# Output copies ahead of products at block seams, filter loads entered in another order, and a constant table in two parts

## The chip, the cores and the metric

One Trainium2 chip, one of its cores. The metric is the device time of one execution in microseconds (us), as the median of several; the lower the better. A profile of one execution of each kernel was taken as well.

## The reference

A frequency-domain mixing layer (a two-dimensional transform of `x`, an elementwise product with a learned complex filter, the transform back) is followed by RMS normalisation and a SwiGLU feed-forward without bias. Cut to what matters:

- `x` is 8 batches of 3008 rows (64 x 47) of 256 columns in single precision; the output has 24064 rows of 256.
- mix: transform, times `filt_r + i filt_i`, transform back, real part;
- norm: `y / sqrt(mean(y^2) + 1e-6) * moe_rms_g`;
- feed-forward: `(silu(y @ w_gate) * (y @ w_val)) @ w_out`.

## The kernel before

In the views PE is TensorE, PEld its weight load, DVE VectorE, ACT ScalarE, POOL GpSimd and SP SyncE; PSUM is the memory that matmuls write their sums to, here in banks.

The feed-forward fills TensorE: each block (batch `b`, `m`) is 12 "slots", one for each 128 columns of the hidden layer. The transforms of the *next* batch are cut into small units, which are put into the slots: stage A (`a_unit`), stage B with the filter products (`b_unit`, and for most units two half-swaps, `swap_unit`), the inverse (`bi_unit`), the normalisation (`n_unit`, `sq_unit`, `q_unit`). Where a unit stands in a slot decides its place in the order of each engine:

```python
def at(slot, fn, *a):
    todo = {q_unit: late, swap_unit: pre}.get(fn, plan).setdefault(slot, [])
    ...
for i in range(len(items) + 4):
    for fn, a in pre.get(i, ()):   fn(*a)       # half-swaps
    if i < len(items):             gv(*items[i])     # gate and value of slot i: 4 matmuls, silu, product hh
    for fn, a in plan.get(i, ()):  fn(*a)       # most units
    if 2 <= i < len(items) + 2:    down(*items[i - 2])   # output matmuls of slot i - 2
    for fn, a in late.get(i, ()):  fn(*a)
```

`down` of a block's last slot, which falls in a slot that is 1 modulo 12 (the "seam"), also copies the finished output out of PSUM: ScalarE one half, VectorE the other. The next block's matmuls into the same bank wait for these copies.

After batch 0, stage B has one PSUM bank. Its readers are, in this order, the product `s1` and the two half-swaps; the second half-swap frees the bank for the next unit:

```python
def b_unit(b, i, ps=None):
    if ps is None:
        ps = b_mm(b, i)                     # 2 matmuls into the single bank "mb"
    ...
    if summed(b, i):
        nc.vector.tensor_tensor(out=s1, in0=ps, in1=f1, op=ALU.mult)
        return
    eng.tensor_tensor(out=s1, in0=ps, in1=f1, op=ALU.mult)
    eng.tensor_tensor(out=s2, in0=ps, in1=f2, op=ALU.mult)

def swap_unit(b, i, h):                     # at slots s0 + 1 (h = 0) and s0 + 2 (h = 1)
    if h:
        nc.vector.tensor_tensor(out=s2[a], in0=ps[e], in1=f2[e], op=ALU.mult)
    else:
        nc.vector.scalar_tensor_tensor(out=s2[a], in0=ps[e], scalar=-1.0, in1=f2[e], ...)
    if h:
        nc.gpsimd.tensor_tensor(out=s, in0=s1, in1=s2, op=ALU.add)
```

Inverse units, stage A and most of the normalisation share another single bank, "mx". The kernel's eight banks are all in use (gate 2, value 2, output 2, "mx", "mb").

The start, where the loads are issued. `x` is cast on its way and is issued by GpSimd, in eight pieces; the real filters are issued by SP once GpSimd has zeroed the half of `fr` that lies under them:

```python
nc.sync.dma_start(tb, tab["tb"])            # constants, 224 KB
nc.sync.dma_start(wbp, tab["wbp"])
for c in range(NXC):
    x_load(0, c)                            # two loads each, by GpSimd
nc.gpsimd.memset(fi[0][HALF:P], 0.0)
nc.gpsimd.memset(fr[0][0:HALF], 0.0)
...
for c in range(4):
    f_load(c, 0, nc.sync)                   # real filters: 4 issues for c = 0
    f_load(c, 1, nc.gpsimd if c < 3 else nc.sync)   # imaginary filters
```

Of the kernel before, what the change touches and what calls it, by code (L numbers as in the profile page):

```python
# [11 lines left out]
FP16 = mybir.dt.float16  # L12
# [8 lines left out]
P = 128  # L21
# [3 lines left out]
JT = DFF // P  # L25
# [13 lines left out]
def _make_tables():  # L39
    n2 = np.arange(N2)  # L40
    wa = np.zeros((P, P))
    wai = np.zeros((P, P))
    for h in range(2):
        for k2 in range(K2):
            c = np.cos(2 * np.pi * ((n2 * k2) % N2) / N2)
            s = np.sin(2 * np.pi * ((n2 * k2) % N2) / N2)
            r = slice(h * 64, h * 64 + 64)
            wa[r, h * 64 + k2] = c
            wai[h * 64 + k2, r] = c * (1.0 if k2 == 0 else 2.0)
            if k2 == 0:  # L50
                alt = 1.0 - 2.0 * (n2 % 2)
                wa[r, h * 64 + 32] = alt
                wai[h * 64 + 32, r] = alt
            else:
                wa[r, h * 64 + 32 + k2] = -s
                wai[h * 64 + 32 + k2, r] = -2.0 * s
    n1 = np.arange(N1)
    wb = np.zeros((KR, K2, P))
    wi = np.zeros((P, 1, 2, P))
    re, im = slice(0, N1), slice(SL, SL + N1)  # L60
    for k2 in range(K2):
        for s in range(48):

            if s < 24:
                k = k2 + 64 * s
                sign, q = 1.0, 16 + 2 * s
            else:
                if k2 and s == 36:
                    continue
                j = s - 23 if (s < 36 or not k2) else s - 24  # L70
                k = 64 * j - (k2 if k2 else 32)
                sign, q = -1.0, 1 + 2 * (s - 24)
            th = 2 * np.pi * ((n1 * k) % N) / N
            c, sn = np.cos(th), np.sin(th)
            if k == 0 or k == NF - 1:
                sn = np.zeros(N1)
            if k2:
                wb[re, k2, q] = c
                wb[im, k2, q] = sign * sn
                wb[re, k2, HALF + q] = -sn  # L80
                wb[im, k2, HALF + q] = sign * c
            else:
                src = re if s < 24 else im
                wb[src, k2, q] = c
                wb[src, k2, HALF + q] = -sn
                m = 1.0 if k in (0, NF - 1) else 2.0
                z = np.zeros(N1)
                g = (m * c, -m * sn)
                gr, gi = (g, (z, z)) if s < 24 else ((z, z), g)


                for qq, cols in ((re, 0), (im, 1)):
                    wi[q, 0, 0, qq] = (gr, gi)[cols][0]
                    wi[HALF + q, 0, 0, qq] = (gr, gi)[cols][1]
                    wi[q, 0, 1, qq] = (gr, gi)[cols][1]
                    wi[HALF + q, 0, 1, qq] = (gr, gi)[cols][0]
    f = np.float16
    wf = np.zeros((P, K2, P))
    wf[:, 1:, 0:KR] = wb[:, 1:].transpose(2, 1, 0)
    wf[:, 0] = wi[:, 0, 0]  # L100
    wf = (wf * S_INV_B).astype(f)
    ws = np.concatenate([wf[HALF:P], -wf[0:HALF]], 0)
    wai = (wai * S_INV_A).astype(f)
    r = np.arange(KR)
    to_row = (r % 2) * SL + (r // 2 % 2) * H + r // 4
    pm = np.zeros((KR, P))
    pm[r, to_row] = 1.0
    k = np.arange(P)
    ph = (k % 2) * 64 + (k // 2 % 2) * 32 + k // 4
    tb = np.zeros((P, 7, P), f)  # L110
    tb[:, 0] = wa
    tb[:, 1] = np.eye(P)
    tb[0:KR, 2] = pm * S_INV_B
    tb[:, 3] = wf[:, 0]
    tb[:, 4] = ws[:, 0]
    tb[:, 5] = wai[ph]
    tb[:, 6] = wa[:, ph]
    return {"tb": tb, "wb": wb.astype(f), "wbp": wb[to_row].astype(f)}


@with_exitstack
def kernel(
# [11 lines left out]
    nc = tc.nc  # L134
# [9 lines left out]
    glob = ctx.enter_context(tc.tile_pool(name="glob", bufs=1))  # L144
# [12 lines left out]
    psM = ctx.enter_context(tc.tile_pool(name="psM", bufs=1, space=bass.MemoryType.PSUM))  # L157
    psB = ctx.enter_context(tc.tile_pool(name="psB", bufs=1, space=bass.MemoryType.PSUM))

    tb = glob.tile([P, 7, P], FP16)  # L160
    wa, ident, wai, wa2 = (tb[:, i, :] for i in (0, 1, 5, 6))
    pm = tb[0:KR, 2, :]
    sgn = glob.tile([P, 1], FP32)
    wi = glob.tile([P, 2, K2, P], FP16)
# [58 lines left out]
        return fr[c][:, r:r + n, :], fi[c][:, r:r + n, :]  # L223

    def wi_at(q, k):
        return wi[:, q, k, :] if k else tb[:, 3 + q, :]

    def b_mm(b, i):
        ps = bank(3 if b else (0, 3, 4, 5)[i % 4], "psb").rearrange("p (a d) -> p a d", a=2)
# [9 lines left out]
        return ps  # L239

    def summed(b, i):
        return b > 1 or b == 1 and i in (6, 7, 10, 11, 14, 15)

    def b_unit(b, i, ps=None):
        if ps is None:
            ps = b_mm(b, i)
        f1, f2 = filt(2 * i, 2)
        if b:
            s1 = late_p["sp"].tile([P, 2, D], FP16, tag="s1", name="s1")
            s2 = late_p["sp"].tile([P, 2, D], FP16, tag="s2", name="s2")  # L250
            if summed(b, i):
                nc.vector.tensor_tensor(out=s1, in0=ps, in1=f1, op=ALU.mult)  # L252
                st[b]["s"][i] = (s1, s2, ps, f2)
                return
        elif i % 2:
            s1 = hp.tile([P, 512], FP16, tag="sg", name="sg").rearrange("p (a d) -> p a d", a=2)
            s2 = hhs[(i // 2) % 4].rearrange("p (a d) -> p a d", a=2)
        else:
            ss = xnp.tile([P, 2, 512], FP16, tag="xn", name="ss")
            s1, s2 = (ss[:, e, :].rearrange("p (a d) -> p a d", a=2) for e in range(2))  # L260
        eng = nc.vector
        if (i in (3, 5, 8, 12)) if b else (i in (3, 7, 9, 12)):
            eng = nc.gpsimd
            v = yp.tile([P, 2, 512], FP32, tag="y", name="v")
            v = v[:, 0, :].rearrange("p (a d) -> p a d", a=2)
            nc.scalar.activation(out=v, in_=ps, func=AXT.Copy)
            ps = v
        eng.tensor_tensor(out=s1, in0=ps, in1=f1, op=ALU.mult)
        eng.tensor_tensor(out=s2, in0=ps, in1=f2, op=ALU.mult)  # L269
        st[b]["s"][i] = (s1, s2)  # L270
# [229 lines left out]
    def f_load(c, e, eng):  # L500
        lo = 1 if c == 0 else 0
        src, t, p0 = ((filt_r, fr[c], 0), (filt_i, fi[c], HALF))[e]
        eng.dma_start(t[p0 + 16:p0 + 63:2, :, :].rearrange("p a d -> p (a d)"),
                      raw(src, c * KC, [[64 * D, 24], [1, KC * D]]))
        for g in range(2):
            eng.dma_start(t[p0 + 1 + 24 * g:p0 + 24 + 24 * g:2, lo:KC, :],
                          raw(src, 64 * (1 + 11 * g) - c * KC - lo,
                              [[64 * D, 12], [-D, KC - lo], [1, D]]))
        if c == 0:
            eng.dma_start(t[p0 + 1:p0 + 48:2, 0, :], raw(src, 32, [[64 * D, 24], [1, D]]))  # L510
# [122 lines left out]
    with tc.manual_schedule():  # L633
# [18 lines left out]
        for c in range(NXC):  # L652
            x_load(0, c)
        nc.gpsimd.memset(fi[0][HALF:P], 0.0)
        nc.gpsimd.memset(fr[0][0:HALF], 0.0)
        nc.vector.memset(aT[:, 2 * H:, :], 0.0)
        nc.vector.memset(ones, 1.0)
# [6 lines left out]
            nc.sync.dma_start(gsb, moe_rms_g.rearrange("(a p) -> p a", p=P))  # L664
        for c in range(4):
            f_load(c, 0, nc.sync)
            f_load(c, 1, nc.gpsimd if c < 3 else nc.sync)

        warm_up(14, 1)
        for g in range(4):  # L670
# [130 lines left out]
        pre, plan, late = {}, {}, {}  # L801

        def at(slot, fn, *a):
            todo = {q_unit: late, swap_unit: pre}.get(fn, plan).setdefault(slot, [])
            if fn == sq_unit:
                todo.insert(0, (fn, a))
            else:
                todo.append((fn, a))

        def norm_plan(b, m, s0, s1, r):  # L810
            for dh in range(2):
                at((s0, s1)[dh], n_unit, b, m, dh)
                at((s0, s1)[dh] + 1, sq_unit, b, m, dh)
            steps = (q_unit, rho_load, xn_unit)
            if halved(b, m):
                at(s1 + 2, fold_unit, b, m)
                r = (4, 8, 12)
            if (b, m) in by_matmul:
                steps = (q_unit, scale_split, scale_apply)
            for d, fn in zip(r, steps):  # L820
                at(s1 + d, fn, b, m, *((3,) if fn == scale_apply else ()))
# [9 lines left out]
        for b in range(1, B):  # L831
# [6 lines left out]
            if b == 1:  # L838
                a_at = [8, 9, 9, 10, 10, 11, 11, 12, 12, 13, 13, 14]
                on_dve = (2, 4, 6, 8, 10)  # L840
                b_at = [22 + 7 * i // 4 for i in range(16)]
                lag, t4_at = 4, 55
                n_at, n_step = [58, 62, 66, 86, 95, 107], 3
            elif b == 2:
                a_at = [51, 52, 53, 53, 54, 54, 57, 57, 58, 59, 60, 61]
                on_dve = (0, 1, 3, 5, 7, 8, 9, 10, 11)
                b_at = [71 + 3 * i for i in range(16)]
                lag, t4_at = 5, 123
                n_at = [127 + 8 * m for m in range(6)]
            elif b == 3:  # L850
                b_at[0] += 1
                a_at = [77, 78, 80, 81, 83, 84, 92, 93, 101, 102, 104, 105]
# [72 lines left out]
```

## Time and profile before

| | |
|---|---|
| median of 4 runs | 893.5 us (892.68 to 894.44) |
| span of the profiled core | 890.6 us |
| TensorE waits for the VectorE output copy | 3.0 us, 6 times |
| ScalarE begins its first copy of the real filters | 20.99 us |
| TensorE's granted clock | full from 4 to 888 us |

From the page of the profiled execution, busy time and share of the span of each engine:

```profile
PE 873.5 (98%) x6258; PEld 559.4 (63%) x6258; DVE 681.5 (77%) x1091; ACT 625.1 (70%) x1068; POOL 435.6 (49%) x392
...
L276 DVE TENSOR_TENSOR s<-psb,fi 64x512 f16<-64x512 f32 x102 | 69.8, 684 | 3.1
```

TensorE (PE) is busy 98%: a change to VectorE's (DVE) order can only be worth the few TensorE gaps that it closes. The second line is the second half-swap: 102 times, 0.684 us each; VectorE hardly ever waits ahead of it (3.1 us in all).

### The profile page before, as it was taken

How to read it: one execution, taken by the hardware profiler on the slowest of the kernel's cores; microseconds unless marked ns; L12 is line 12 of the kernel's file. 1: busy time of each engine (PE TensorE's matmuls, PEld its weight loads, DVE VectorE, ACT ScalarE, POOL GpSimd, SP SyncE). 2: the span in 40 equal slices, each digit the busy share in tenths (PEclk: the TensorE clock that was granted, in tenths of full speed). 3: DMA queues.
4: the chain of work that ended last, by engine and by line, in shares of the span. 5: the costliest groups of instructions: out<-in, count | busy, mean ns of one | idle time of the engine just before them, and what ended most of it. 6: DMA issues, size and time to landing. Idle time of an engine off the chain costs nothing.

```text
span 890.6 us, 17468 instructions
## 1 busy us (share of the span) xinstructions
PE 873.5 (98%) x6258; PEld 559.4 (63%) x6258; DVE 681.5 (77%) x1091; ACT 625.1 (70%) x1068; POOL 435.6 (49%) x392
## 2 busy tenths in 40 slices
PE   8799999999999999999999999999999999999997
PEld 5666666666666666666666666666666666666556
DVE  7866787889987877888688787888878887555555
ACT  7877657677677766877677766787657765676444
POOL 7843830656427661677236662376515762155300
PEclk9999999999999999999999999999999999999999
DMA  8696726675663456335645247233352232222202
GB/s 196 122 196 156 157 67 207 143 158 110 162 159 89 101 111 185 107 90 113 159 119 132 86 81 199 80 94 90 88 163 72 67 90 61 85 66 49 72 24 48
DMA packets 80095, 101.44 MB, mean 114 GB/s; under 512 B 8108, under 2 KB 56684, under 8 KB 79560
## 3 DMA queue, kind: packets, MB, share of 16 engines
q1 hardware_dynamic: 69688, 84.23, 34.8%
q0 software_dynamic: 10240, 15.96, 11.4%
q8 instruction: 49, 0.80, 0.4%
q14 instruction: 38, 0.31, 0.1%
q10 hardware_dynamic: 80, 0.13, 0.1%
HBM read 67.67 MB, written 46.78 MB: 129 GB/s over the span
## 4 chain that ended last, share of the span: by engine, by line
PE 87%; issue 4%; DVE 2%; ACT 2%; DMA 2%; POOL 2%; SPq 0%; ACTq 0%; POOLq 0%; DVEq 0%
PE po L462 26%; PE pg L443 25%; PE pv L443 25%; PE psi L291 3%; PE psb L238 3%; PE psn L323 2%; PE psa L203 2%; DMA fr<-in_filt_r_dram 1%; DVE o L469 1%; ACT fr L516 1%; DVE hh L448 1%; DMA rb<-r_tmp 1%; ACT gT L578 1%; PE psq L352 0%; POOL xc L188 0%
## 5 line engine op out<-in xcount | busy, mean ns | idle before, releaser
L448 DVE TENSOR_TENSOR hh<-pv,sg 128x512 f16<-128x512 f32 (+2 forms) x588 | 392.9, 670 | 190.2 <-ACT sg L447 77.6
L447 ACT ACTIVATE sg<-pg 128x512 f16<-128x512 f32 (+2 forms) x588 | 340.9, 580 | 227.5 <-PE pg L443 217.8
L462 PE MATMUL po<-wo,hh 128*128 128x256 f16 x2244 | 343.2, 272 | 3.8 <-DVE o L469 3.0
L443 PE MATMUL pv<-xn,wv 128*128 128x512 f16 (+2 forms) x1176 | 339.6, 370 | 0.0
L443 PE MATMUL pg<-xn,wg 128*128 128x512 f16 (+2 forms) x1176 | 339.5, 370 | 0.0
L462 PEld LDWEIGHTS <-hh 128*128 128x128 f16 x2256 | 216.4, 98 | 99.0 <-issue 5.3
L282 POOL TENSOR_TENSOR s<-s,s 128x512 f16<-128x512 f16 x102 | 117.9, 1157 | 237.5 <-DVE s L276 165.6
L443 PEld LDWEIGHTS <-wv 128*128 128x128 f16 x1176 | 114.9, 98 | 128.8 <-issue 0.3
L419 POOL TENSOR_TENSOR xn<-y,rb 128x1024 f16<-128x1024 f32 (+1 forms) x45 | 126.0, 2801 | 44.9 <-DMA rb<-r_tmp 37.7
L443 PEld LDWEIGHTS <-wg 128*128 128x128 f16 x1176 | 111.4, 98 | 13.0 <-issue 0.3
L358 POOL TENSOR_TENSOR rho<-u,mhalf 128x4 f32<-128x4 f32 (+1 forms) x48 | 49.1, 1022 | 63.5 <-DVE u L356 63.1
L276 DVE TENSOR_TENSOR s<-psb,fi 64x512 f16<-64x512 f32 x102 | 69.8, 684 | 3.1
L296 ACT ACTIVATE t<-psi 96x512 f16<-96x512 f32 x112 | 66.4, 593 | 8.1 <-PE psi L291 2.7
L278 DVE SCALAR_TENSOR_TENSOR s<-psb,fi 64x512 f16<-64x512 f32 x102 | 70.7, 693 | 1.4
L252 DVE TENSOR_TENSOR s<-psb,fr 128x512 f16<-128x512 f32 x102 | 69.4, 681 | 0.0
L329 ACT ACTIVATE y<-psn,gsb 128x512 f32<-128x512 f32 (+1 forms) x94 | 63.8, 679 | 7.8 <-PE psn L323 0.5
L343 POOL TENSOR_TENSOR sq<-sq 128x512 f16<-128x512 f16 (+1 forms) x35 | 39.6, 1133 | 35.9 <-ACT sq L335 35.9
L335 ACT ACTIVATE sq<-psn 128x512 f16<-128x512 f32 (+1 forms) x94 | 54.8, 583 | 0.0
L208 ACT ACTIVATE t<-psa 128x512 f16<-128x512 f32 x70 | 41.8, 597 | 5.6 <-PE psa L203 2.4
L291 PE MATMUL psi<-s,wi 128*128 128x256 f16 x236 | 44.1, 273 | 0.0
L238 PE MATMUL psb<-t,wb 96*128 96x256 f16 x224 | 43.0, 272 | 0.5 <-DVE s L269 0.5
L323 PEld LDWEIGHTS <-t 128*128 128x128 f16 x368 | 28.4, 98 | 20.6 <-issue 0.4
(104 smaller groups left out, 523.1 us busy)
## 6 DMA issues: line engine op xcount, KB each, us to landing
out_dram<-o SPq DMA_DIRECT2D x83, 256.0 KB
xc<-in_x_dram POOLq DMA_DIRECT2D x56, 192.0 KB, 5.8
z_tmp<-t SPq DMA_DIRECT2D x28, 384.0 KB
t<-z_tmp SPq DMA_DIRECT2D x28, 384.0 KB
g_tmp<-t SPq DMA_DIRECT2D x56, 192.0 KB
rb<-r_tmp SPq DMA_DIRECT2D x41, 256.0 KB
t<-g_tmp SPq DMA_DIRECT2D x21, 384.0 KB
t<-g_tmp SPq DMA_DIRECT2D x7, 320.0 KB
```

The lines of the kernel that those rows point to most:

```text
L238: nc.tensor.matmul(ps[:, u, :], w[:, k, :], t, start=True, stop=True)
L252: nc.vector.tensor_tensor(out=s1, in0=ps, in1=f1, op=ALU.mult)
L276: nc.vector.tensor_tensor(out=s2[a], in0=ps[e], in1=f2[e], op=ALU.mult)
L278: nc.vector.scalar_tensor_tensor(out=s2[a], in0=ps[e], scalar=-1.0, in1=f2[e], op0=ALU.mult, op1=ALU.mult)
L282: nc.gpsimd.tensor_tensor(out=s, in0=s1, in1=s2, op=ALU.add)
L291: nc.tensor.matmul(ps[:, u, :], wi_at(q, 2 * i + u), ss[q][:, u, :], start=(q == 0), stop=(q == n - 1))
L296: nc.scalar.activation(out=st[b]["t3"][c][:, 2 * r:2 * r + 2, :], in_=ps[0:KR], func=AXT.Copy)
L419: nc.gpsimd.tensor_tensor(out=xv, in0=yv, in1=rv.unsqueeze(1).to_broadcast([P, 2, n, P]), op=ALU.mult)
L443: nc.tensor.matmul(ps[:, 0:w], wt[:, dt_, ts(jt, P)], xn[:, dt_, :], start=(dt_ == 0), stop=(dt_ == 1))
L447: nc.scalar.activation(out=sg[:, 0:w], in_=pg[:, 0:w], func=AXT.Silu)
L448: nc.vector.tensor_tensor(out=hh[:, 0:w], in0=pv[:, 0:w], in1=sg[:, 0:w], op=ALU.mult)
L462: nc.tensor.matmul(po[s4 // per][:, s4 % per, :], hh[:, ts(s4, P)], wo[:, jt, :], start=(jt == 0 and s4 % per == 0), stop=(jt == JT - 1 an ...
```

## The change

Its intent: at the seams, let the output copies go ahead of the stage A, stage B and swap work, so that the next block's matmuls are not held; let `x` enter the DMA queues before the real filters; fetch only what is needed at once of the constants. Cut to the core (the table's packing and its readers follow the same split):

```diff
-    return {"tb": tb, "wb": wb.astype(f), "wbp": wb[to_row].astype(f)}
+    return {"tb": tb, "tc": tc, "wb": wb.astype(f), "wbp": wb[to_row].astype(f)}
...
-        return b > 1 or b == 1 and i in (6, 7, 10, 11, 14, 15)
+        return b > 1 or b == 1 and i in (6, 7, 10, 11, 14)
...
-        if (i in (3, 5, 8, 12)) if b else (i in (3, 7, 9, 12)):
+        if (i in (3, 5, 8, 12, 15)) if b else (i in (3, 7, 9, 12)):
...
         nc.gpsimd.memset(fi[0][HALF:P], 0.0)
+        f_load(0, 1, nc.gpsimd)
         nc.gpsimd.memset(fr[0][0:HALF], 0.0)
...
             f_load(c, 0, nc.sync)
-            f_load(c, 1, nc.gpsimd if c < 3 else nc.sync)
+            if c == 0:
+                nc.sync.dma_start(tk, tab["tc"])
+            else:
+                f_load(c, 1, nc.gpsimd if c < 3 else nc.sync)
...
         def at(slot, fn, *a):
-            todo = {q_unit: late, swap_unit: pre}.get(fn, plan).setdefault(slot, [])
+            at_seam = slot % JT == 1 and fn in (a_unit, b_unit, swap_unit)
+            todo = late if at_seam or fn == q_unit else pre if fn == swap_unit else plan
+            todo = todo.setdefault(slot, [])
...
-                r = (4, 8, 12)
+                r = (5 if (b, m) == (2, 1) else 4, 8, 12)
...
-                b_at = [22 + 7 * i // 4 for i in range(16)]
+                b_at = [22 + 7 * i // 4 + (i == 1) for i in range(16)]
```

More of the change, by code (lines that the diff above doesn't have):

```diff
@@ L109, in _make_tables @@
     ph = (k % 2) * 64 + (k // 2 % 2) * 32 + k // 4
-    tb = np.zeros((P, 7, P), f)
+    tb = np.zeros((P, 3, P), f)
+    tc = np.zeros((P, 4, P), f)
     tb[:, 0] = wa
@@ L113, in _make_tables @@
     tb[0:KR, 2] = pm * S_INV_B
-    tb[:, 3] = wf[:, 0]
-    tb[:, 4] = ws[:, 0]
-    tb[:, 5] = wai[ph]
-    tb[:, 6] = wa[:, ph]
-    return {"tb": tb, "wb": wb.astype(f), "wbp": wb[to_row].astype(f)}
+    tc[:, 0] = wf[:, 0]
+    tc[:, 1] = ws[:, 0]
+    tc[:, 2] = wai[ph]
+    tc[:, 3] = wa[:, ph]
+    return {"tb": tb, "tc": tc, "wb": wb.astype(f), "wbp": wb[to_row].astype(f)}
 @with_exitstack
@@ L158 @@
     psB = ctx.enter_context(tc.tile_pool(name="psB", bufs=1, space=bass.MemoryType.PSUM))
-    tb = glob.tile([P, 7, P], FP16)
-    wa, ident, wai, wa2 = (tb[:, i, :] for i in (0, 1, 5, 6))
+    tb = glob.tile([P, 3, P], FP16)
+    tk = glob.tile([P, 4, P], FP16)
+    wa, ident = (tb[:, i, :] for i in (0, 1))
+    wai, wa2 = (tk[:, i, :] for i in (2, 3))
     pm = tb[0:KR, 2, :]
@@ L225, in wi_at @@
     def wi_at(q, k):
-        return wi[:, q, k, :] if k else tb[:, 3 + q, :]
+        return wi[:, q, k, :] if k else tk[:, q, :]
     def b_mm(b, i):
```

## The prediction

> **What bounds the kernel now.** I read the busy table by stretches first, then the TensorE waits, then the chain of waits for the start, then the timeline around the places where a block ends. In the table the columns are the stretch, its length, and the busy time of TensorE, weight loads, VectorE, ScalarE and GpSimd.
>
> ```profile
> 0.00:50.00 50.00, 42.10 (x498) 29.95 (x499) 39.38 (x68) 40.59 (x60) 39.78 (x51) 1.00 0.83 162
> 122.00:246.00 124.00, 122.32 (x857) 77.63 (x856) 105.58 (x170) 87.48 (x152) 57.19 (x58) 1.00 0.59 147
> 493.00:615.00 122.00, 122.00 (x848) 78.01 (x847) 99.47 (x158) 90.63 (x156) 64.53 (x54) 1.00 0.42 110
> ```
>
> TensorE is full from 50 us on; in the middle batches no idle is left at all. Idle TensorE is in the start (7.9 us of 50) and in the first batches. What it waits for after the start:
>
> ```profile
> PE po L462 <- DVE o L469: 3.0, 6, 0.8
> PE psb L238 <- DVE s L269: 0.5, 2, 0.3
> PE psq L352 <- POOL sq L343: 0.5, 1, 0.5
> PE po L462 <- DVE hh L448: 0.3, 1, 0.3
> ```
>
> These sums are low, because the modelled end of one matmul covers part of the next gap. I measured the gaps from start to start instead: a 256-column matmul follows the last after 0.109 us, a 512-column one after 0.216. Beyond that, block ends lose 0.17 us (at 70.8 us), 0.76 (90.3), 0.98 (111.6), 0.84 (131.8), 0.46 (150.9), 0.56 (166.0) and 0.42 (240.8); the wait for a sum of squares loses 0.66 (273.4), two waits for the stage B bank 0.45 (84.4) and 0.38 (97.1). The last batch loses 0.2 to 0.3 at each of its block ends with nothing in VectorE's way, and from batch 3 to there I find none over 0.06. So all that the seams can give is about 5 us, 0.5%.
>
> One such seam, in the timeline (start, duration, engine, work):
>
> ```profile
> 110.26 0.68 DVE L269 TENSOR_TENSOR s<-psb,fi 128x512 f16<-128x512 f32 x1
> 110.40 0.38 PE L462 MATMUL po<-wo,hh 128*128 128x256 f16 x2
> ...
> 110.86 0.68 DVE L469 COPY o<-po 128x512 f32<-128x512 f32 x1
> ...
> 111.59 0.38 PE L462 MATMUL po<-wo,hh 128*128 128x256 f16 x2 [0.81 <-DVE o L469]
> ```
>
> The output block was ready at 109.3, but its VectorE copy stands behind two filter products (L268, L269) and begins at 110.86. The next block's third matmul could have begun at 110.40 + 0.22 = 110.62 and begins at 111.59.
>
> The start, from the chain of waits (start, duration):
>
> ```profile
> 5.92 1.82 POOL fi L654
> 7.79 1.81 POOL fr L655
> 9.62 0.95 SPq L503
> ...
> 12.29 8.59 DMA fr<-in_filt_r_dram
> 20.99 1.16 ACT fr L516 x2
> ```
>
> Two GpSimd memsets, then the real filters' load, then its copy to the other half; from there ScalarE and VectorE are full until about 38 us, so a later landing of fr moves everything behind it.
>
> **What the Trainium skill says.** "PSUM — Partial Sum Buffer", section Engine vs sequencer instructions: the ScalarE, VectorE and GpSimd queues are strict FIFO. The seam above agrees: a ready copy waits for 1.5 us behind products that TensorE does not need. "TensorE: Matmul & The Clock Gate", section Back-to-back issue gap, gives N/2.4 + 2.5 ns for a warm isolated matmul, 216 ns at 512 columns and 109 at 256; the trace has these spacings throughout, so the full stretches are at their limit. "Perfetto Trace Analysis", section Optimization Strategy: find the gaps of the most-contended engine and what its semaphores wait for; a repeating bubble can mean too few PSUM buffers. That matters below: stage B has one bank. "DMA: Bandwidth & Descriptors", section Queues, rings and completion order: each DMA engine takes turns between the queues with work. The packets agree in part: fr was issued from 9.62, its first packet ran at 13.71, when x was nearly through (last x packet 14.27).
>
> **The change part by part.** *Output copies first.* At a slot that is 1 modulo 12 the stage A units, stage B units and swaps now come after the output matmuls and copies. The instruction order shows which move: stage A at slots 13 and 61, stage B products at 25 and 37, and the second half-swap (L276) at 73, 85, 97, 109 and 121. Batch 1's unit 15 (48, swap at 49) becomes two GpSimd products fed by a ScalarE copy, with two more stage-C matmuls (0.22 us). Unit 1 goes from slot 23 to 24, and one sum of squares is read one slot later, behind its fold.
>
> Gains, replaying each place with its own durations (VectorE instructions follow each other at about 0.61 us there):
> - slot 37: copy at 109.06 + 0.61 = 109.67, done by 110.4, before 110.62: all 0.98 us;
> - slots 23 to 25: 0.45 + 0.76 go, but unit 2 now waits for unit 1's products, about 0.22: 0.99;
> - slot 49: copy done at about 131.0 instead of 131.7: 0.73, less 0.22 for the extra matmuls: 0.51;
> - slot 61: 0.46; slot 13: about 0.1, since the next ScalarE copy of the pair comes later; sum of squares 0.66.
> Sum 3.7 us.
>
> Losses: the five L276. Stage B has one PSUM bank after batch 0, L276 is the last reader of it, and at all five places the next stage B unit stands in the very next slot. Slot 85:
>
> ```profile
> 182.43 0.60 ACT L447 ACTIVATE sg<-pg 128x512 f16<-128x512 f32 x1 [0.27 <-PE pg L443]
> 182.56 0.68 DVE L276 TENSOR_TENSOR s<-psb,fi 64x512 f16<-64x512 f32 x1
> ...
> 183.27 0.69 DVE L448 TENSOR_TENSOR hh<-pv,sg 128x512 f16<-128x512 f32 x1
> ...
> 183.88 0.68 DVE L469 COPY o<-po 128x512 f32<-128x512 f32 x1
> ...
> 184.40 0.38 PE L238 MATMUL psb<-t,wb 96*128 96x256 f16 x2
> ```
>
> Here TensorE loses nothing before. After: hh at 183.07 (sg ends 183.03), copy 183.68, L276 184.29 to 184.97, and with the 0.06 us that such a wait took at 84.37 the stage B matmul begins at 185.03, 0.63 late. Slots 97 and 109 have the same picture: 0.62 each. Slot 73: 165.88 instead of 164.96 is 0.92, while the 0.56 of the copy goes: 0.36 lost. Slot 121: 0.85 less 0.42: 0.43 lost. Sum 2.7 us. So the loop gains 3.7 - 2.7 = 1.0 us.
>
> *Filters.* The imaginary filters' four issues (about 2.4 us in the trace, 9.55 to 12.03) move between the two memsets. So the fr memset ends at about 7.75 + 2.45 + 1.85 = 12.05 and SP's load starts 2.4 us later than 9.62. Most of it should be hidden: before, the first fr packet ran 4.1 us after its issue, behind x; wbp's first packet ran 1.5 us after its issue on an idle queue. 12.05 + 1.5 = 13.55, as early as 13.71. The later pieces are tighter: their last issue moves from 12.29 to about 14.7, and their packets ran from 15.8 to about 19. I take the landing as the same to 0.7 us later: +0.3.
>
> *Tables.* The first table shrinks from 224 to 96 KB ahead of wbp: its packets took 0.085 us each, 128 over 16 engines, so some 0.3 to 0.4 us less in front of the 1.1 us wait for wbp. It helps x and so the stage A of batch 0, but fr decides when the products begin. The other 128 KB go between fr's first and second chunk; the copy of the second chunk runs at 25.8, with room. I count -0.3. The start together: 0.
>
> Sum: 893.95 - 1.0 + 0 = about 893.0 us.
>
> **The rivals.**
> 1. *The copies simply come free*: the swaps do not hold stage B. For it: the change names the swaps, and two of the seams that it treats (73, 121) do stand in the list of gaps. Against: the bank's single buffer and the slack of only 1.1 us at slot 85 against a delay of 1.7 us. Then the loop gains the 3.7 and the 0.98 of slots 73 and 121, 4.7 in all: 889.3 us.
> 2. *The start takes it back*: the fr load really enters 2.4 us later and lands 2 us later. For: everything from 21 to 38 us hangs on it, and ScalarE waited for this landing for 0.37 us already. Against: DMA was 0.95 busy from 10 to 20 us, so the order of entry hardly counts. Then +2: 895.0 us.
> 3. *Fetching x first shortens the start*: x free of fr's traffic and behind a shorter table lands perhaps 0.5 us earlier, and fr, undisturbed, too. Then 0.7 us better: 892.3 us.
>
> **Range and chances.** The loop can give from -2.7 (losses alone) to +4.7, the start from +2 to -1. The extremes do not meet often; 890.5 to 895.6 should hold it 8 times in 10. Two per cent is 17.9 us, more than all gaps after 45 us together (some 10) or the idle of the start; so within 2% has 0.98, faster and slower 0.01 each.
>
> **What would show it.** Right: the TensorE wait for o at L469 falls from 3.0 us to under 1; the wait of psb (L238) for s of L276, absent before, appears five times, 0.3 to 0.9 us each, between 165 and 241 us; at 110 us the copy stands ahead of L268; fr's copy by ScalarE still begins within 0.7 us of 20.99. Wrong: no psb wait at these slots (rival 1), or ScalarE's first fr copy after 22.5 us (rival 2) or before 20.5 (rival 3). A change beyond 5 us either way would mean a cause that I have not seen.

## More of the kernel before

Line numbers of the kernel after are three to four higher (L276 is L279 there, L469 is L472, L462 is L465).

## The result, and the profile after

| | before | after |
|---|---|---|
| median | 893.5 us (892.68 to 894.44, 4 runs) | 895.0 us (893.86 to 895.67, 4 runs) |
| ratio after / before | | 1.0015, 95% interval 0.9998 to 1.0033 |
| span of the profiled core | 890.6 us | 893.8 us |

The ratio is the mean time of the one kernel's fast runs over that of the other's in the same rounds, so not quite the ratio of the medians. Within 2%, as expected, but 2 us above the point predicted and on the other side of the kernel before: 1.5 us slower instead of about 0.5 to 1 us faster. The interval of the ratio still includes no difference at all.

Busy time by stretches, kernel after (columns as in the prediction; the last three are the granted TensorE clock, the DMA share and GB/s):

```profile
0.00:50.00 50.00, 40.53 (x461) 29.43 (x462) 36.74 (x63) 38.05 (x55) 35.92 (x45) 0.93 0.75 151
122.00:246.00 124.00, 120.68 (x848) 76.75 (x846) 101.93 (x164) 86.95 (x152) 58.27 (x57) 1.00 0.56 141
```

Both stretches lost TensorE time: 1.6 us in each, and the first shows a clock of 0.93 where it was 1.00. TensorE's waits from 50 us on, kernel after (what waits, for what: us in total, times, longest):

```profile
PE psb L241 <- DVE s L279: 3.3, 5, 0.8
PE po L465 <- DVE hh L451: 0.3, 1, 0.3
PE psb L241 <- DVE s L272: 0.2, 1, 0.2
```

The waits for the output copy (3.0 us, 6 times) and for the sum of squares are gone; five waits of stage B for the second half-swap took their place. Slot 37 after, in the timeline (start, duration, engine, line, work, idle time and releaser in brackets):

```profile
112.65 0.68 DVE L472 COPY o<-po 128x512 f32<-128x512 f32 x1
...
113.25 0.68 DVE L271 TENSOR_TENSOR s<-psb,fr 128x512 f16<-128x512 f32 x1
...
113.38 0.60 PE L465 MATMUL po<-wo,hh 128*128 128x256 f16 x4
```

The copy now stands ahead of the products, and the four output matmuls run through without a wait, where the third waited 0.81 us. Slot 85 after, the counterpart of the place shown in the prediction:

```profile
184.44 0.69 DVE L451 TENSOR_TENSOR hh<-pv,sg 128x512 f16<-128x512 f32 x1 [0.54 <-PE psi L294]
...
185.04 0.68 DVE L472 COPY o<-po 128x512 f32<-128x512 f32 x1
...
185.76 0.68 DVE L279 TENSOR_TENSOR s<-psb,fi 64x512 f16<-64x512 f32 x1
...
186.50 0.38 PE L241 MATMUL psb<-t,wb 96*128 96x256 f16 x2 [0.55 <-DVE s L279]
```

The half-swap (L279) ends at 186.44 and the next stage B matmul, which overwrites the same bank, begins 0.06 us later. From start to start the gap over the usual spacing is 0.715 us here; at the five slots 73, 85, 97, 109 and 121 it is 1.00, 0.72, 0.71, 0.71 and 0.94 us.

The start. The chain of waits of the kernel after (start, duration, what):

```profile
11.41 0.54 POOL fi L513
...
12.00 1.81 POOL fr L659
...
13.82 0.94 SPq L506
...
17.36 6.63 DMA fr<-in_filt_r_dram
...
24.09 1.15 ACT fr L519 x2
```

The real filters' load is issued at 13.82 instead of 9.62, lands at about 24, and ScalarE's copy of it begins 3.10 us later than before (24.09 against 20.99). Why GpSimd's memset of `fr` began only at 12.00 shows in GpSimd's own timeline:

```profile
8.49 0.54 POOL L506 DMA_DIRECT2D fi<-in_filt_i_dram  x1 [0.76 <-DMA xc<-in_x_dram]
9.51 0.66 POOL L509 DMA_DIRECT2D fi<-in_filt_i_dram  x1 [0.47 <-DMA xc<-in_x_dram]
10.49 0.61 POOL L509 DMA_DIRECT2D fi<-in_filt_i_dram  x1 [0.32 <-DMA xc<-in_x_dram]
11.41 0.54 POOL L513 DMA_DIRECT2D fi<-in_filt_i_dram  x1 [0.31 <-DMA xc<-in_x_dram]
```

Each of the four issues of the imaginary filters waits for a piece of `x` to land, although neither touches the other's data. The trace's semaphores explain it: GpSimd's loads take eight completion semaphores in turn; the eight pieces of `x` used all eight, so the next four loads reuse the first four and are issued after these pieces landed (7.90, 9.22, 10.20 and 11.13 us): the first 0.6 us later, the others 0.3.

One thing more: in the stretch before the first block the kernel after was lent half the clock. The same window of both kernels, before first (the kernel after is 3 us behind, so the work in it is not the same; read the clock, third number from the end):

```profile
41.00:45.00 4.00, 3.84 (x51) 3.08 (x50) 2.76 (x7) 2.99 (x6) 2.04 (x3) 1.00 1.21 176
```

```profile
41.00:45.00 4.00, 3.71 (x38) 3.04 (x38) 1.19 (x3) 2.23 (x6) 4.00 (x6) 0.58 0.62 94
```

The clock record of the kernel after has two stretches of half clock, each 3.41 us (from 28.0 and from 41.65 us); that of before has none until 888 us. Following the same instructions in both traces, the shift is 3.10 us from ScalarE's copy on and steady through the products, and grows to 4.15 us while the second of these stretches lasts.

To place the rest, I compared when the first gate product of each block began, after minus before:

| from slot to slot | predicted | measured |
|---|---|---|
| start to slot 0 | 0 | +4.15 |
| 0 to 36 (slots 13, 23 to 25) | -1.09 | -1.17 |
| 36 to 48 (slot 37) | -0.98 | -0.98 |
| 48 to 60 (slot 49) | -0.51 | -0.61 |
| 60 to 72 (slot 61) | -0.46 | -0.46 |
| 72 to 132 (five half-swaps) | +2.66 | +3.10 |
| 132 to 156 (sum of squares) | -0.66 | -0.66 |
| 156 to the end | 0 | 0.0 |

So the loop gains 0.8 us net (predicted 1.0), and the start loses 4.15 us in this trace, which is that of the slowest of the four runs.

### The profile page after: what moved, and what is told of

The parts are those of the page before. It is cut to its first block, busy times and chain, and to the rows that moved or that the text cites. A ratio compares the mean times of both kernels' runs of the same rounds, so it can differ in the third digit from the quotient of the medians.

```text
span 893.8 us, 17474 instructions
## 1 busy us (share of the span) xinstructions
PE 875.8 (98%) x6260; PEld 562.0 (63%) x6260; DVE 679.4 (76%) x1088; ACT 625.9 (70%) x1069; POOL 436.4 (49%) x393
## 4 chain that ended last, share of the span: by engine, by line
PE 88%; issue 4%; DMA 2%; ACT 2%; DVE 2%; POOL 1%; SPq 0%; ACTq 0%; POOLq 0%
PE po L465 26%; PE pg L446 26%; PE pv L446 25%; PE psb L241 3%; PE psi L294 3%; PE psn L326 2%; PE psa L206 2%; DMA xc<-in_x_dram 1%; DVE o L472 1%; DMA fr<-in_filt_r_dram 1%; ACT fr L519 1%; PE psq L355 0%; DVE s L279 0%; ACT gT L581 0%; DMA rb<-r_tmp 0%
## 5 line engine op out<-in xcount | busy, mean ns | idle before, releaser
L279 DVE TENSOR_TENSOR s<-psb,fi 64x512 f16<-64x512 f32 x101 | 69.0, 683 | 3.1
```

## The experiments

Theories to be told apart: *S*, the four issues ahead of GpSimd's memset hold the real filters back and cost the start some us; rival *C*, the loss comes from the table or is the clock's chance; rival *E*, it is the order of the data in the DMA queues. *B*, a half-swap behind a seam holds the single stage B bank; rival *D*, the delay would show elsewhere anyway. *H*, the half clock follows from TensorE's idle time. Every kernel in the table gave correct results. Kernels e1 to e4 ran on one chip (before there: 894.0, 11 runs), e5 to e12 on another (893.1); compare ratios rather than medians across.

| | median us | ratio to before (95%) | ScalarE's first fr copy, us |
|---|---|---|---|
| e1 filters back | 892.73 | 0.9989 (0.9967 to 1.001) | 21.25 |
| e2 swaps in front | 891.54 | 0.9973 (0.9952 to 0.9993) | 23.33 |
| e3 both back | 889.57 | 0.9951 (0.9929 to 0.9973) | 20.63 |
| e4 filters alone | 894.98 | 1.0012 (0.9993 to 1.0032) | 23.55 |
| e5 tables alone | 893.63 | 1.0011 (0.9997 to 1.0024) | 20.65 |
| e6 imaginary filters by ScalarE | 899.22 | 1.0073 (1.0061 to 1.0086) | 27.32 |
| e7 batch 2 shifted | 901.84 | 1.0097 (1.0083 to 1.0111) | 21.15 |
| e8 one piece ahead | 892.60 | 1.0000 (0.9987 to 1.0013) | 23.99 |
| e9 e7 with TensorE kept busy | 900.99 | 1.0088 (1.0074 to 1.0101) | 21.30 |
| e10 e7 with the inverses in place | 888.32 | 0.9952 (0.9938 to 0.9965) | 21.35 |
| e11 e10 with TensorE kept busy | 888.54 | 0.9954 (0.9940 to 0.9967) | 20.67 |
| e12 x in five loads | 907.03 | 1.0158 (1.0145 to 1.0170) | 35.22 |

### e1: the filters' order as before, the rest of the change kept

```diff
         nc.gpsimd.memset(fi[0][HALF:P], 0.0)
-        f_load(0, 1, nc.gpsimd)
         nc.gpsimd.memset(fr[0][0:HALF], 0.0)
...
             if c == 0:
                 nc.sync.dma_start(tk, tab["tc"])
-            else:
-                f_load(c, 1, nc.gpsimd if c < 3 else nc.sync)
+            f_load(c, 1, nc.gpsimd if c < 3 else nc.sync)
```

> Theory S (the four issues of the imaginary filters ahead of GpSimd's memset of fr hold the real filters' load back, and that costs about 4 us at the start; the rest of the change gains some 0.8 us): the fr load is issued at 9.6 us again instead of 13.8, ScalarE's first copy of fr begins at 20.7 to 21.3 us instead of 24.1, block by block the shift against the kernel before is within 0.5 us at slot 0 and -0.3 to -1.3 us from slot 156 on, and the time is 0.3 to 1.3 us below the kernel before, so about 892.7. Rival C (the start's 4 us are not the filters' order, but the later fetch of half of the tables or a chance of the TensorE clock): the shift at slot 0 stays at 3 to 4 us and the time stays 1 to 2 us above the kernel before.

Measured: the fr load is issued at 9.60 us. ScalarE's timeline:

```profile
21.25 1.16 ACT L519 ACTIVATE fr<-fr 64x512 f32<-64x512 f32 x2 [0.64 <-DMA fr<-in_filt_r_dram]
```

The shift at slot 0 is +1.29 rather than under 0.5: +0.26 to the copy, and 1.03 more under a half-clock stretch from 39.0 us. From slot 156 on it is +0.50, outside the -0.3 to -1.3, by just this stretch; the median, 892.73, is as expected. The loop's shares are those of the kernel after to 0.1 us (five waits of psb for s, 3.3 us; net gain 0.79). So the order of the filters' loads, not the loop or the table, makes the difference between 895.0 and 892.7 (medians of different sessions; e2 against e3 below is a pair of one session).

### e2: the second half-swaps ahead of the block again

```diff
-            at_seam = slot % JT == 1 and fn in (a_unit, b_unit, swap_unit)
+            at_seam = slot % JT == 1 and fn in (a_unit, b_unit)
```

> The second half-swaps go back ahead of the block, the start stays as in the kernel after. Theory B (the swaps behind the seam hold the single stage B bank): the TensorE waits of psb for s disappear at slots 73, 85, 97, 109 and 121, the waits for the output copy come back at slots 73 (0.5 to 0.6 us) and 121 (0.4), and nowhere else; the loop gains 2.1 us against the kernel after (3.1 less about 1), so 893.0 if the kernel after gives 895.0. Rival D (the later swaps do not cost, the time comes back through VectorE anyway, since the same work must be done before the next block): the gaps turn up at other places of the same stretch, and the time stays within 0.7 us of the kernel after.

Measured, the largest of TensorE's waits from 50 us on:

```profile
PE po L465 <- DVE o L472: 0.7, 2, 0.4
```

The five psb waits are gone and two waits for the output copy are back, with gaps of 0.56 us at slot 73 and 0.42 at slot 121. From slot 72 to 132 the shift against the kernel before stays at -0.53: no loss and nothing turned up elsewhere. Theory B holds, D falls. The median, 891.54, is 1.5 us below what I had, by a slip of mine: I had taken the 1 us of slots 73 and 121 off the bank's 3.1 us, which is net of it already (five gaps of 4.08 us in all, less 0.98). 895.0 less 3.1 is 891.9.

### e3: both taken back

The edits of e1 and e2 together.

> Both of the above taken back; only the units of stages A and B behind the seam, unit 15 on GpSimd, the fold and the split table remain. If S and B hold and add: start as before, no loss between slots 72 and 132, so the kernel before less 3 to 3.5 us: about 890.2. If the gains of the loop were given back elsewhere (a later wait): less than 2 us below the kernel before.

Measured: 889.57, 4.4 us below the kernel before on the same chip (3 to 3.5 were expected), no run of it (888.75 to 890.36) above a run of e2 (890.43 to 892.57). The loop alone gives 3.9 us (shift +0.65 at slot 12, -3.24 from slot 168 on). The parts add: e2 minus e3, the filters, is 2.0 us; e1 minus e3, the swaps, 3.2 us (3.1 in the table of slots); e3 plus both is 894.7, and the kernel after had 895.0.

### e4: the kernel before with the filters' order alone

```diff
         nc.gpsimd.memset(fi[0][HALF:P], 0.0)
+        f_load(0, 1, nc.gpsimd)
         nc.gpsimd.memset(fr[0][0:HALF], 0.0)
...
-            f_load(c, 1, nc.gpsimd if c < 3 else nc.sync)
+            if c:
+                f_load(c, 1, nc.gpsimd if c < 3 else nc.sync)
```

> The kernel before with the filters' order alone. Theory S: fr's load is issued at 13 to 14 us, its copy begins 2.5 to 3.5 us later than 20.99, and the whole kernel is 2.5 to 4.5 us slower than the kernel before: about 897. Rival C: within 1 us of the kernel before. A part of it may show as a TensorE clock that drops to half in the first 50 us, since TensorE then idles longer: up to 1 us more.

Measured, ScalarE's timeline:

```profile
23.55 1.15 ACT L516 ACTIVATE fr<-fr 64x512 f32<-64x512 f32 x2 [2.71 <-DMA fr<-in_filt_r_dram]
```

Issued at 13.64, copied 2.56 us later than before, and 2.5 us is the shift in every block to the end. Rival C falls for the trace. By the times, though, it is only 1.0 us (the ratio says 1.1, with 1 inside its interval), less than the 2.5 expected, and by the times alone rival C would stand; the eleven runs of before scatter from 892.17 to 898.38, and the traced run of before was one of the faster ones. I take 1 to 2.3 us as the cost of this part.

### e5: the kernel before with the split table alone

The table's edit of the diff above, with the imaginary filters' load left where it was.

> The kernel before with the split table alone. The prediction took 0.3 us for it; the two versions with the filters' order as before and the split table had ScalarE's first fr copy at 21.25 and 20.63 against 20.99, so no clear gain. Theory: within 0.5 us of the kernel before, the fr copy between 20.6 (where ScalarE is free) and 21.3. Rival (the smaller first table brings x and wbp in earlier and the start gains): the copies of stage A end 0.3 us earlier or more, and the kernel is 1 us faster or more.

Measured: 893.63 against 893.05, ratio 1.0011 with 1 inside the interval; the shift of the traced run is -0.16 to -0.19 in every block, its fr copy at 20.65. The split table does nothing that these runs can show.

### e6: ScalarE issues the four pieces

```diff
         nc.gpsimd.memset(fi[0][HALF:P], 0.0)
-        f_load(0, 1, nc.gpsimd)
...
             zero(fi[c][HALF:P])
+        f_load(0, 1, nc.scalar)
```

> The kernel after, but ScalarE issues the four pieces of the imaginary filters' first chunk, behind its own zeroing; they still enter before the real filters do. Theory S in the form 'GpSimd is held at these issues, and its memset of fr behind them': fr's load is issued at 9.6 us again instead of 13.6 to 13.8, and ScalarE's copy of fr begins by 21.5 instead of 23.3 to 24.1, although the order on the wires is that of the kernel after; ScalarE's own first work may slip by up to 2.4 us, of which I expect under 1 us to reach the products. Rival E ('it is the order of the data, fi ahead of fr, that makes fr land late'): fr lands as late as in the kernel after, 23.3 us or more, though it was issued at 9.6.

Measured: fr is issued at 9.60, and its first packet ran at 13.77 us (before 13.71, after 16.23): with GpSimd not held, it enters as before although the imaginary filters enter first. ScalarE's copy doesn't show the landing here, since ScalarE itself came late. Its timeline:

```profile
11.75 1.99 ACT L614 ACTIVATE wi<-pst,sgn 128x384 f16<-128x384 f32 x3 [3.99 <-issue]
```

It spent 4.0 us on the four issues, not the 2.4 that I had allowed, its first copies began at 11.75 instead of 7.78, and TensorE, waiting for them, ran at half clock from 10.23 to 20.47 us. So the 6 us lost are another loss than the one studied. That GpSimd's hold is the cause of the late issue is shown.

The landing itself stands in the trace, in the completion semaphores that the copy waits for. In the runs where `fr` alone sets the copy's start, the copy follows the last of the four pieces by 0.1 us:

| | four pieces of `fr` issued from, us | last of them landed, us |
|---|---|---|
| before | 9.62 | 20.88 |
| e1 | 9.60 | 21.15 |
| after | 13.82 | 23.98 |
| e4 | 13.64 | 23.44 |
| e6 | 9.60 | 23.96 |
| e8 (below) | 10.82 | 23.88 |

In e6 `fr` was issued on time and still landed as late as in the kernel after, which is what rival E had forecast (23.3 us or more). So an issue on time is not enough to bring the landing back. E is not shown either: e6 puts the imaginary filters on a third queue beside the other two, and GpSimd issues the second chunk of them 2.9 us earlier than before (9.53 against 12.46), so more data moves next to `fr`. What is shown is that the filters' order costs the start; how much of that is the late issue and how much the data beside `fr` is open.

### e7: stage B of batch 2 a slot earlier

On top of e1: whole units instead of half-swaps fall on the seams. The first unit of batch 3 moves a slot earlier with them.

```diff
-                b_at = [71 + 3 * i for i in range(16)]
+                b_at = [70 + 3 * i for i in range(16)]
...
-                b_at[0] += 1
...
-                at(s0 + lag - (b == 3 and i == 0), bi_unit, b, i)
+                at(s0 + lag, bi_unit, b, i)
```

> The filters' order as before, the swaps still at the seam by rule, but stage B of batch 2 starts a slot earlier, so that at the seams a whole unit (its matmuls and the first product) goes behind the output copy, and no swap falls on a seam; the next unit is two slots away. Theory B (only a swap directly ahead of the next stage B unit costs): no TensorE wait of psb between slots 72 and 132, and no wait for the output copy at slots 73 and 121 either, so the loop gains the 0.98 us more than the version with the swaps in front: 888.6 against its 889.57. Rival (products behind a seam are late for the inverse five slots on, or the earlier stage B waits for its data from memory): a new wait of psi or psb of 0.5 us or more, and 889.5 or above.

Measured: 901.84, a clear miss. The two largest of TensorE's waits:

```profile
PE psa L206 <- ACT t L299: 4.8, 7, 0.7
PE psi L294 <- ACT sq L338: 4.5, 6, 0.7
```

As expected, no wait of stage B for a half-swap and none for the output copy is left in batch 2. But the inverse units hang on `b_at` and moved a slot earlier too, next to units of stage A and of the normalisation that use their bank "mx": 13 new gaps of 0.84 to 0.91 us each between 170 and 243 us, 11.4 us in all. I had looked at one single bank and forgotten the other. e10 tests this.

### e8: one of the four pieces ahead

```diff
-        f_load(0, 1, nc.gpsimd)
+        f_load(0, 1, nc.gpsimd, (0,))       # the 24 x 2048 piece; the other three as before the change
```

> The kernel after with one of the four pieces (24 x 2048) left ahead of the fr memset and three behind it, where all four were before. Theory S with the waits for completions: each issue on GpSimd comes about 0.3 to 0.6 us after the landing of the x piece eight issues back; the first then at 8.5, so the memset runs 9.1 to 10.9, the fr load is issued at about 11.0 and its copy begins at 21.5 to 22.3, between 21.0 (none ahead) and 23.3 to 24.1 (four); 893.3 against 895.0. If instead the first of the four alone causes the loss: fr at 13 us or later.

Measured: the memset began at 9.0 and fr was issued at 10.82, as expected, and the median is 892.60, 0.7 below what I expected. The medians show no clear cost of one piece ahead: the ratio to the kernel before is 1.0000 (0.9987 to 1.0013), that of e1, with none ahead, 0.9989 (0.9967 to 1.001). ScalarE's timeline of the traced run does not fit, though:

```profile
23.99 1.15 ACT L522 ACTIVATE fr<-fr 64x512 f32<-64x512 f32 x2 [3.38 <-POOL fi L526]
```

The expectation was 21.5 to 22.3. This run took 895.04, the slowest of its five (the others 891.88 to 893.21), so its copy may not be that of a usual run. The releaser named does not produce what this copy reads; by the semaphores the copy waited for `fr`, whose last piece landed at 23.88 us (table under e6), though its first packet ran at 13.89, as in the kernel before, and it was issued only 1.2 us later. What made it land late is open. With none ahead, eight traces have the copy between 20.63 and 21.35; with four ahead, three traces between 23.33 and 24.09.

### e9: e7 with TensorE kept busy in batch 0's stage B

```diff
-        if b == 0 and i > 3:
+        for _ in range((8 if i < 6 else 4) if b == 0 and i > 3 else 0):
             nc.tensor.matmul(ps[:, 0, :], wz[:, 0:P], wz[:, 0:D], start=True, stop=True)
```

> The shifted version with 44 more dummy matmuls of 0.109 us ahead of batch 0's stage B units 4 to 15 (eight ahead of 4 and 5, four ahead of the rest, instead of one each), 4.8 us of TensorE time in a stretch where it idles for about a third. Theory H (TensorE's half clock for 3.41 us between 26 and 45 us, which cost about 1.0 us in three of the six traces, follows TensorE's idle time there): no half-clock record before 880 us, mean clocks of 0.999 or 1.000 in all runs, less spread, and the median 0.3 to 0.7 us below the shifted version. Rival (the windows come whatever TensorE does, or the dummies delay the inverses): clocks of 0.995 to 0.998 in some runs still, or a time equal or longer by up to 1.5 us.

Measured: mean clocks 1.000, 0.999, 0.999, 1.000 and 1.000, against 0.998, 0.997, 0.995 and 0.995 in e7, and no half-clock stretch before 899 us in the trace. The median is 0.85 us below e7's.

### e10: the shift, with the inverses left at their slots

```diff
-                lag, t4_at = 5, 123
+                lag, t4_at = 6, 123
```

> The shifted version again, with batch 2's inverse units kept at the slots where they stood (six slots after stage B instead of five). Theory M (the 8 to 9 us that the shifted version lost are twelve TensorE waits for the one bank that inverse units, stage A of batch 3 and the normalisation share, because the inverses moved a slot into them): the psi and psa waits of 0.84 to 0.91 us between slots 72 and 132 vanish, and the version reaches 888.6 to 889.2, at or below the one with the swaps in front (889.57). Rival (the earlier stage B itself is what costs): it stays above 893.

Measured: 888.32. No wait of psi, of psb for a half-swap or of po for a copy is left between slots 72 and 132; the 13 gaps are gone, so e7's loss was the bank "mx". From slot 12 to the end the loop gains 4.76 us, what rival 1 of the prediction had counted (4.7) for seams whose copies come free. It beats both kernels: 4.7 us below the kernel before (ratio 0.9952), level with e3 within the intervals.

### e11: e10 with the dummy matmuls of e9

> The same with the 44 dummy matmuls in batch 0's stage B, which had kept the mean clock at 0.999 to 1.000 in all five runs. Theory H again: clocks of 0.999 or 1.000, a spread under 1.5 us, and a median 0 to 0.8 us below the same version without them (the dummies delay the inverses by part of what the clock gives). If the median is above it, the dummies cost more than the half clock did.

Measured: clocks of 1.000 four times and 0.999 once (e10: 1.000, 0.995, 0.998, 0.999), a spread of 1.7 us (888.11 to 889.83; under 1.5 was expected) against 3.0, and a median of 888.54, level with e10. So theory H holds for the clock in both pairs, ten runs without a half-clock stretch ahead of the end as far as the mean tells; but the dummies stand ahead of real matmuls: in the traces of both e9 and e11 the shift grows by 0.79 us at one of the inverses' copies (at 32.6 us in the kernel before), about what a half-clock stretch costs, and nothing is left of the gain in the median.

### e12: x in five loads

```diff
         for h in range(2):
             ...
+        if b == 0 and not last:     # both halves in one load of 128 partitions
+            nc.gpsimd.dma_start(t.rearrange("p a d -> p (a d)"),
+                                bass.AP(tensor=x.tensor, offset=x[b].offset + c * XC * D,
+                                        ap=[[H * D, 2], [N1 * D, 64], [1, XC * D]]))
```

> The kernel after, with batch 0's x in five loads instead of eight (three of 128 partitions, two for the last chunk). Theory W (the four issues of the imaginary filters are slow in the kernel after, 8.5 to 12.0 us instead of the 2.4 us that they take unhindered, because each waits until the load eight issues back on GpSimd's queue has landed): with five x loads the first three have none to wait for and the fourth an early one; x itself is issued 1.5 us sooner. So the four issues take 2.3 to 2.6 us right behind the memset, GpSimd's fr memset starts by 9.0 to 10.2 us instead of 12.0, and the fr load is issued by 10.9 to 12.1 instead of 13.6 to 13.8. Rival (the issues are slow because the queue is full, whatever it was filled with): they still end at 11.5 us or later.

Measured: the kernel is 14 us slower than the one before, for a reason of my making (below), but the question is answered. GpSimd's timeline:

```profile
7.40 0.54 POOL L510 DMA_DIRECT2D fi<-in_filt_i_dram  x1 [0.29 <-POOL fi L661]
7.95 1.28 POOL L513 DMA_DIRECT2D fi<-in_filt_i_dram  x2
21.95 0.55 POOL L517 DMA_DIRECT2D fi<-in_filt_i_dram  x1 [12.72 <-DMA xc<-in_x_dram]
```

Loads six to eight on GpSimd's queue follow each other at 0.55 and 0.66 us, unhindered; the ninth waits 12.72 us, until the first load has landed (21.66 us), and is issued 0.29 us later. The wait is for the load eight issues back, whatever it carries: theory W. By the times alone, a queue that holds eight loads would look the same; what tells them apart is the wait recorded with each of these issues, which names the semaphore of the load eight back. The expected issue of fr at 10.9 to 12.1 failed (24.37) because that first load landed so late. The Trainium skill, "DMA: Bandwidth & Descriptors", section Why a DMA increments its semaphore by 16 and not by 1, says that a load is spread over the largest number of engines, up to 16, that divides the slowest dimension of both patterns (with exceptions for some loads issued by GpSimd); my source began with a dimension of 2. The trace agrees in direction: from 10 to 20 us the DMA share was 0.47 and 88 GB/s, against 0.95 and 206 before. No run tests it.

## Why the prediction was right or wrong

*Which view bounds the kernel, and how little the seams can give:* right. About 5 us was the most; e10, which gets nearly all of it, gained 4.76 from slot 12 on.

*Gains of the loop:* right place by place (table above), with 3.9 us for the 3.7 predicted.

*Losses by the half-swaps:* right in mechanism, slots and number; 3.1 us for 2.7. The half-swap began 0.72 us after the copy (slot 85), not the 0.61 that I had replayed, at each of the five seams. e2 shows that they are the swaps' alone. Rival 1, that the swaps come free, was wrong.

*Tables, -0.3:* nothing that the runs show (e5), an error within the noise.

*Filters, +0.3:* this step failed, and rival 2, "the start takes it back", is what happened. Two terms were mis-sized. The four issues were taken at 2.4 us from the trace before, where for three of the four the piece of `x` in question had landed; in the new place they wait for these landings one by one and last from 8.49 to 11.95 us, so that fr was issued at 13.6 to 13.8, not 12.05. And the delay was to be hidden by DMA work that was going on anyway ("the order of entry hardly counts"); in the three traces with this order ScalarE's copy begins 2.3 to 3.1 us later. The first packet of `fr`, reckoned at 13.55 us, ran at 16.23. (The 1.5 us in that sum was not that of an idle queue: the packets of `tb` ran ahead of `wbp` on it. `tb` itself, issued at 0.74, had its first packet at 1.74 us. And the turns between queues that the prediction cites do not show while `x` loads: in the trace before no packet of `fr` ran from its issue at 9.62 until 13.71.) Which part of the later landing comes from the late issue and which from the data moved beside `fr` stays open (e6, e8). In the medians the part costs 2.0 us (e2 against e3), 2.3 (after against e1, from different sessions) and 1.1 (e4).

*The sum:* -0.8 from the loop and +1.1 to +2.3 from the start give +0.3 to +1.5; the medians differ by 1.5 (895.0 less 893.5). The sign of the point predicted was wrong; the result is inside the range of 890.5 to 895.6 since rival 2 had set its upper end.

*Not foreseen:* the clock. Half-clock stretches of 3.41 us, or twice that, fall somewhere between 25 and 46 us in many runs, by their mean clocks also in runs of before (0.992 to 1.000 there). One that falls on the part that TensorE sets cost 0.84 us (e3, from 30.97), 1.03 (e1) and 1.04 (after), one among the products cost nothing (e4: 6.8 us of half clock from 26.25, and the shift stays 2.5). That explains 1.04 us of the traced run of the kernel after. It may be a part of the scatter of 1 to 3 us: of the eleven runs of before on the first chip the three fastest have mean clocks of 0.999 and 1.000, the two slowest 0.995 and 0.992. The Trainium skill, "TensorE: Matmul & The Clock Gate", Part 1: The HAM clock gate, describes it: activity is watched in a "free-running 4096-cycle activity window" of about 3.4 us, so where it falls is chance; the records agree (3.413 us, clock 0.5). That TensorE's idle time brings it on is what e9 and e11 speak for: none of their ten runs has a mean clock under 0.999, of the eight of e7 and e10 six have. Whether the kernel after has more of it than the one before is not settled: their mean clocks overlap.

*Still open:* how much of the later landing of `fr` is its late issue and how much the data moved beside it. In e6 and e8 it landed at 23.96 and 23.88 us with an issue at 9.60 and 10.82.

## What to carry to other kernels

Before work is moved behind a critical copy, look for who waits for that work: an instruction that is the last reader of a single-buffered bank cannot move without moving the next writer, and a unit that is shifted takes its followers along into other single banks (e7 against e10). Before a load is moved ahead of other work on its issuing engine, see what that issue itself will wait for; here it was the load eight issues back, and everything behind it on the engine, a memset and with it another queue's load, waited too. And read when the load lands, not only when it is issued: in e6 the issue was back in time and the landing was not. Differences of 1 to 2 us in single traces need their clock record read first.

## What the Trainium skill lacked or had wrong

- "DMA: Bandwidth & Descriptors" (none of its sections has it): in these programs a load issued by GpSimd waits until the load eight issues back on the same queue has landed, because eight completion semaphores are used in turn. Issues that take 0.55 to 0.66 us unhindered were spread over 3.5 us (8.49 to 11.95), and one waited 12.72 us.
- The same page, section Rules for kernel authors, advises one 128-partition transfer instead of two of half the partitions. In e12, with a source pattern whose outermost dimension was 2, the first merged load landed at 21.66 us, where before the first two half loads, with the same rows, had landed by 8.58 us. The condition on the outermost dimension stands in another row of the same table ("Use all 16 engines"); it belongs beside this rule. That it is the cause here is not tested.
- The same page, section Issuing engines are not separate DMA queues, calls the sequencer's time to initiate a load "usually small relative to the DMA itself". That agrees (before, each piece of `fr` took 0.76 to 0.95 us to issue and 7.6 to 9.0 us from issue to landing), but the section gives no duration, and issues in a row add up: four held ScalarE for 4.0 us (e6) and SP for 3.4 us (9.62 to 13.05 in the trace before).
- "TensorE: Matmul & The Clock Gate", section Back-to-back issue gap, gives 131 ns as the sustained spacing of 512-column matmuls and says that the isolated formula over-counts. Here the sustained spacing is the formula's 216 ns throughout.
